# Loading the gate and mix vectors first, longer steps for the softmax sums, and an even pace for the attention

## The chip, the cores and the metric

The kernel runs on 1 core of a Trainium2 chip. Its time is the device time of one execution in microseconds (us); several executions are run and their median is given. All engines of the core work at once: TensorE (PE: matmuls; PEld: its weight loads), VectorE (DVE), ScalarE (ACT), GpSimd (POOL) and SyncE (SP), which in this kernel issues every DMA.

## The reference, cut to what matters

```python
def _attn_ref(q, k, v, cap):                     # 4 batches, 12 heads, 448 positions, 64 wide
    scores = 1.0 / np.sqrt(q.shape[-1]) * np.matmul(q, k.transpose(0, 1, 3, 2))
    scores = cap * np.tanh(scores / cap)
    scores = scores - np.max(scores, axis=-1, keepdims=True)
    attn = np.exp(scores)
    attn = attn / (np.sum(attn, axis=-1, keepdims=True) + 1e-09)
    return np.matmul(attn, v)

def _moe_ref(x, w_val, conv_w, w_out):           # x: 4 x 448 x 768, five taps
    gate = 1.0 / (1.0 + np.exp(-causal_conv(x, conv_w)))
    return gate * (x @ w_val) @ w_out

def _moe2_ref(x, mu_k, mu_r, w_k, w_v, w_r):     # 768 -> 1024 -> 768
    xk = mu_k * x + (1.0 - mu_k) * x_prev
    xr = mu_r * x + (1.0 - mu_r) * x_prev
    k = np.maximum(xk @ w_k, 0.0)
    return 1.0 / (1.0 + np.exp(-(xr @ w_r))) * (k * k @ w_v)

reference = _moe2_ref(_moe_ref(_attn_ref(...)))
```

`causal_conv` stands for the sum over five taps of `conv_w[k] * x` shifted by k positions; `x_prev` is x shifted by one. The weights and `conv_w` arrive as 64-bit numbers, which the kernel narrows to 32 bits.

## The kernel before, in words

**Number format.** Every dense operand is split in two parts, a rounded one and the rest (`split_hi`, `split_lo`), and a product takes three matmuls: high by high, high by low, low by high.

**Attention** goes by pairs of heads, 24 pairs, six per batch. A pair is cut into six pieces (`piece`): piece 0 computes the first two slots of the scores, their tanh and exp, and their sum over slots on GpSimd (`add_up`); piece 1 multiplies the pair before with v (`pv`, copied into `x_f` by ScalarE); pieces 2 and 3 transpose and split the next pair's q and k (`qk_T`, on VectorE or, later, ScalarE and VectorE); piece 4 computes the other two slots; piece 5 adds up the pair before over positions on TensorE (`sums`).

**The chain of the sums.** `sums` (L290) leaves the softmax sums in `rows`; from there they go by DMA into a tile with 128 partitions (`rec<-rows`), VectorE adds a guard (L300) and inverts (L301, `invert`), a DMA writes the reciprocals to DRAM (`recd<-rec`), another reads them back spread over partitions (`R<-recd`, `load_R`), and GpSimd multiplies `x_f` by them (`divide`, L369). Then `x_split` makes the two parts of x, and five taps (`tap`: the first on ScalarE, L379, four on VectorE, L385) and one sigmoid per batch (L389) make the gate. `post(n, ...)` puts each of these n steps later; a step is a piece of attention or a half layer of dense work.

**Order.** Nothing is scheduled at run time: the program's order on each engine is kept (`in_order`). The first 10 pairs run by themselves, with the narrowing and splitting of `w_val` between their pieces (`make_val`). Then the batches go through the dense layers `val` and `out`, 24 half layers of 9 matmuls per batch; behind each half layer the function `behind_first` adds `PACE[b]` to a credit and runs one more piece of attention for each whole credit. The 86 pieces that are left after the first 10 pairs are worked off in this way. Weights of `val`, `out` and `r` are split once, written to DRAM and streamed from there (`wp`), four half layers ahead. With the fourth batch the buffers of the first stage are given back, and `w_k` and `w_v` are made; the second stage is the dense layers `r`, `k`, `v` for each batch.

**Vectors.** `vectors` (L652) loads `conv_w` and the two mix vectors, narrows `conv_w` in five VectorE operations (`narrow`: L444 to L448), transposes all of them on TensorE (`pc`, L666) and copies them to `vecT`. It is called before pair 1. Its tiles come from rings of two buffers, which the slices of the weights use too:

```python
vec = pools["mk"].tile([128, DM], F32, tag="wr", name="vec")[0:8]
c64 = pools["mk"].tile([128, DM, 2], I32, tag="x64", name="c64")
...
make_val(0)
...
for i in range(FIRST):
    if i == 1:
        vectors()
```

## Time and profile before

| what | value |
|---|---|
| time, median of 3 runs (lowest to highest) | 879.13 us (877.95 to 880.84) |
| the profiled execution's own time | 877.56 us |
| its span, first to last instruction | 875.8 us |
| mean granted clock of TensorE | 0.938 |
| busy: PE, PEld, DVE, ACT, POOL | 752.7, 583.8, 480.0, 443.1, 343.6 us |
| instructions | 10699 |
| DMA traffic | 135.50 MB, mean 155 GB/s |
| chain that ended last, by engine | PE 45%, DVE 16%, DMA 16%, ACT 10%, issue 6%, POOL 4%, SPq 2% |

The busy share of an engine over the whole span mixes stages with different limits. The chain that ended last follows the last instruction back to what released it, step by step; a DMA in it is a transfer that something waited for. Where a row shows "idle before" with a releaser, the engine stood still for that long until the one named was done. A matmul's end is modelled, and spans on POOL are rough.

### The profile page before, as it was taken

The page shows a single profiled execution, that of the slowest core. Times are in us where ns is not written, and L with a number is a line of the kernel's source. Part 1 is how long each engine was busy: PE and PEld are TensorE (multiplying, and loading weights), DVE is VectorE, ACT ScalarE, POOL GpSimd, SP SyncE. Part 2 cuts the span into 40 slices and gives each one's busy share as a digit, 9 for nine tenths or more (in the row PEclk, how much of TensorE's full clock was granted, in tenths as well). Part 3 has the DMA queues.
Part 4 walks back from the last instruction along what each step waited for, and adds up shares of the span by engine and source line. Part 5 has one row for each costly group of instructions (what it writes and reads, how often), then busy time and mean ns, then how long its engine had stood idle before and what let it go on. Part 6 is the DMA issues. An engine that isn't in the chain of part 4 may idle for free.

```text
span 875.8 us, 10699 instructions
## 1 busy us (share of the span) xinstructions
PE 752.7 (86%) x3798; PEld 583.8 (67%) x3798; DVE 480.0 (55%) x653; ACT 443.1 (51%) x673; POOL 343.6 (39%) x259
## 2 busy tenths in 40 slices
PE   3676689869789898779899977888999999999996
PEld 2333345536456655545789756768999999999995
DVE  3577887759945746464525756886423332333310
ACT  4475869647575757676232445543443343335311
POOL 2296777636744636576023646774000000000000
PEclk8687879979889999999989999999999999999999
DMA  7264533564647577754668898333720390145001
GB/s 177 66 178 133 148 91 90 140 192 146 205 154 242 182 206 231 236 166 130 209 219 305 292 311 302 108 118 99 229 74 21 85 286 15 43 124 168 1 21 47
DMA packets 148029, 135.50 MB, mean 155 GB/s; under 512 B 78071, under 2 KB 127223, under 8 KB 147966
## 3 DMA queue, kind: packets, MB, share of 16 engines
q1 hardware_dynamic: 147966, 134.72, 51.4%
q8 instruction: 32, 0.52, 0.2%
q14 instruction: 31, 0.25, 0.1%
HBM read 109.35 MB, written 25.25 MB: 154 GB/s over the span
## 4 chain that ended last, share of the span: by engine, by line
PE 45%; DVE 16%; DMA 16%; ACT 10%; issue 6%; POOL 4%; SPq 2%; POOLq 0%; ACTq 0%; DVEq 0%
PE psd L631 37%; PE pv L286 3%; DMA rec<-rows 3%; DVE wr L447 3%; DMA recd<-rec 3%; PE s L244 3%; DVE gate L385 3%; ACT t L246 2%; DVE wr L446 2%; ACT t L253 2%; SPq L142 2%; DMA of<-out 2%; DVE wr L448 1%; DMA wp<-pdout 1%; DMA R<-recd 1%
## 5 line engine op out<-in xcount | busy, mean ns | idle before, releaser
L631 PE MATMUL psd<-blk,wp 128*128 128x448 f32 x1296 | 292.3, 381 | 20.9 <-ACT r L568 6.3
L631 PEld LDWEIGHTS psd<-blk,wp 128*128 128x128 f32 x1296 | 246.6, 194 | 66.5 <-issue 21.3
L631 PE MATMUL psd<-blk,wv 128*128 128x448 f32 x576 | 124.6, 372 | 1.3 <-ACT blk L170 1.1
L170 ACT CAST blk<-f 128x448 fp32r<-128x448 f32 x104 | 59.0, 567 | 128.5 <-DVE f L592 52.8
L631 PE MATMUL psd<-blk,wk 128*128 128x448 f32 x576 | 118.5, 366 | 4.3 <-DVE f L576 4.2
L385 DVE SCALAR_TENSOR_TENSOR gate<-xf,vecT,gate 128x445 f32<-128x445 f32 (+2 forms) x96 | 95.0, 992 | 41.3 <-ACT gate L379 40.7
L631 PEld LDWEIGHTS psd<-blk,wk 128*128 128x128 f32 x576 | 107.9, 188 | 14.3 <-DVE f L576 5.8
L631 PEld LDWEIGHTS psd<-blk,wv 128*128 128x128 f32 x576 | 107.9, 190 | 10.5 <-ACT blk L170 1.4
L175 DVE TENSOR_TENSOR blk<-f,blk 128x448 fp32r<-128x448 f32 x104 | 76.3, 733 | 40.9 <-ACT blk L170 40.8
L271 POOL TENSOR_TENSOR acc<-acc,t 128x896 f32<-128x896 f32 x24 | 54.5, 2271 | 73.5 <-ACT t L253 73.4
L244 PE MATMUL s<-qh,kh 64*128 64x448 f32 x192 | 46.3, 474 | 39.9 <-DVE kh L172 23.9
L246 ACT ACTIVATE t<-s 128x896 f32<-128x896 f32 x72 | 64.0, 917 | 32.0 <-PE s L244 32.0
L253 ACT ACTIVATE t<-t 128x1792 f32<-128x1792 f32 (+1 forms) x48 | 72.5, 1511 | 1.2
L268 POOL TENSOR_TENSOR acc<-t 128x896 f32<-128x896 f32 x24 | 54.2, 2258 | 45.2 <-ACT t L253 27.5
L286 PE MATMUL pv<-t,vn 128*64 128x448 f32 x288 | 70.0, 627 | 0.1
L274 POOL TENSOR_TENSOR acc<-acc,t 64x448 f32<-64x448 f32 x48 | 64.2, 1338 | 3.6
L592 DVE SCALAR_TENSOR_TENSOR f<-of,vecT,prev 128x448 f32<-128x448 f32 x48 | 33.5, 698 | 49.3 <-ACT prev L590 45.8
L244 PEld LDWEIGHTS s<-qh,kh 64*128 64x128 f32 x192 | 19.9, 199 | 59.0 <-issue 19.2
L445 POOL TENSOR_SCALAR wr<-wr 128x384 f32<-128x384 f32 (+1 forms) x28 | 53.5, 1909 | 11.7 <-ACT wr L443 11.6
L576 DVE TENSOR_TENSOR f<-psd,kr 128x448 f32<-128x448 f32 x32 | 19.9, 622 | 61.8 <-ACT kr L574 61.8
L369 POOL TENSOR_TENSOR xf<-xf,R 128x448 f32<-128x448 f32 x24 | 29.5, 1230 | 61.3 <-DMA R<-recd 60.4
L447 DVE SCALAR_TENSOR_TENSOR wr<-x,wr 128x768 int32<-128x768 int32 (+2 forms) x46 | 48.7, 1058 | 1.4
(79 smaller groups left out, 881.1 us busy)
## 6 DMA issues: line engine op xcount, KB each, us to landing
wp<-pdr SPq DMA_DIRECT2D x48, 384.0 KB
wp<-pdval SPq DMA_DIRECT2D x42, 384.0 KB
wp<-pdout SPq DMA_DIRECT2D x36, 384.0 KB
of<-out SPq DMA_DIRECT2D x48, 224.0 KB
x<-in_moe_w_k_dram SPq DMA_DIRECT2D x16, 384.0 KB
x<-in_moe_w_v_dram SPq DMA_DIRECT2D x12, 512.0 KB
qn<-in_q_dram SPq DMA_DIRECT2D x48, 112.0 KB
kn<-in_k_dram SPq DMA_DIRECT2D x48, 112.0 KB
```

Of the source, the lines that this page charges most:

```text
L170: eng.copy(dst, src)
L175: eng.tensor_tensor(dst, src, hi.bitcast(F32), ALU.subtract)
L244: nc.tensor.matmul(ps[:, h], lhsT=a[r, keys[h]], rhs=x[r], start=(m == 0), stop=(m == 2))
L246: nc.scalar.activation(out=t_t[i][:, at:at + 2], in_=ps, func=ACTF.Tanh, scale=reg_t)
L253: nc.scalar.activation(out=a, in_=a, func=ACTF.Exp, scale=reg_e)
L268: eng.tensor_tensor(acc_t[i], t[:, 0:2], t[:, 2:4], ALU.add)
L271: eng.tensor_tensor(acc, acc, t[:, 4:6], ALU.add)
L274: eng.tensor_tensor(acc[r, h], acc[r, h], t[r, 6], ALU.add)
L286: nc.tensor.matmul(ps[64 * h:64 * h + 64], lhsT=w, rhs=t[:, at], start=(n == 0), stop=(n == 3))
L385: eng.scalar_tensor_tensor(g[:, k:], x[:, :S - k], w, g[:, k:], ALU.mult, ALU.add)
L447: lambda: D.scalar_tensor_tensor(mi, hw, -(1 << 30), mi, ALU.bitwise_and, ALU.bitwise_or),
L631: nc.tensor.matmul(ps, lhsT=lhsT, rhs=x[xp], start=(kk == 0 and m == 0), stop=(kk == kb - 1 and m == 2),)
```

## The change

It has three parts.

1. The vectors are loaded after pair 1's q and k and pair 0's v, ahead of pair 2's q, k and v and of the first slice of `w_val`. The five narrowing operations are issued two at a time after the pieces of pair 0, and the transposes after piece 4 of pair 1. The rings of two buffers stay as they are.
2. The chain of the sums: `invert` 5 steps after `sums` instead of 4, `recd<-rec` 7 instead of 6, `R<-recd` 9 instead of 8, `divide` 13 instead of 11, `x_split` 15 instead of 14, the taps from 15 on instead of 13, the sigmoid 20 instead of 18. `rec<-rows` stays at 2.
3. `PACE` is 1.45, 1.45, 1.5 instead of 1.55, 1.55, 3.0.

An assertion is added that a pair is divided when `x_split` takes it; it issues nothing.

```diff
@@ -21,7 +21,7 @@
 
 MAKE_IN = 46
 
-PACE = (1.55, 1.55, 3.0)
+PACE = (1.45, 1.45, 1.5)
 
 SPLIT_AT = (14, 15, 16, 21, 22, 23)
 
@@ -301,8 +301,8 @@
             nc.vector.reciprocal(r, r)
 
         post(2, lambda: dma(out=r, in_=rows[0::64]))
-        post(4, invert)
-        post(6, lambda: dma(out=rec_d[i].rearrange("h s -> (h s)").rearrange("(p n) -> p n", n=NS), in_=r))
+        post(5, invert)
+        post(7, lambda: dma(out=rec_d[i].rearrange("h s -> (h s)").rearrange("(p n) -> p n", n=NS), in_=r))
         prep(*divmod(i, NP))
 
     def shifted(i):
@@ -354,7 +354,7 @@
 
 
     again = [False]
-    x_f, x_R, x_blk, gate_t, gated = {}, {}, {}, {}, set()
+    x_f, x_R, x_blk, gate_t, gated, divided = {}, {}, {}, {}, set(), set()
 
     def prep(b, hp):
 
@@ -367,6 +367,7 @@
 
         def divide():
             nc.gpsimd.tensor_tensor(x_f[i], x_f[i], x_R.pop(i), ALU.mult)
+            divided.add(i)
 
         def tap(k):
             if hp == 0 and k == 0:
@@ -390,14 +391,14 @@
             gated.add((b, again[0]))
 
         if not again[0]:
-            post(8, load_R)
-            post(11, divide)
+            post(9, load_R)
+            post(13, divide)
         if again[0] or b == 0:
-            at(14, x_split, b, hp)
+            at(15, x_split, b, hp)
         for k in range(TAPS):
-            at(13 + k, tap, k)
+            at(15 + k, tap, k)
         if hp == KD - 1:
-            at(13 + TAPS, sigmoid)
+            at(15 + TAPS, sigmoid)
 
     def new_blk():
         return blk_p.tile([128, 2, S], F32R, tag="blk", name="blk")
@@ -412,6 +413,7 @@
         return t[:, 0], t[:, 1]
 
     def x_split(b, hp):
+        assert again[0] or b * NP + hp in divided
         x_blk[b, hp] = split_blk(x_f[b * NP + hp], nc.scalar, engines["PD"[hp % 2]], 0 if again[0] else 1)
 
 
@@ -650,24 +652,28 @@
                 pend.append((b, o))
 
     def vectors():
+
         vec = pools["mk"].tile([128, DM], F32, tag="wr", name="vec")[0:8]
+        ops = []
         if conv_w.dtype == I64:
             c64 = pools["mk"].tile([128, DM, 2], I32, tag="x64", name="c64")
             dma(out=c64[0:TAPS].rearrange("p n two -> p (n two)"), in_=conv_w.bitcast(I32))
+            ops = narrow(c64[0:TAPS], vec[0:TAPS])
         else:
             dma(out=vec[0:TAPS], in_=conv_w)
         dma(out=vec[TAPS:TAPS + 1], in_=mu_k.unsqueeze(0))
         dma(out=vec[TAPS + 1:TAPS + 2], in_=mu_r.unsqueeze(0))
-        if conv_w.dtype == I64:
-            for fn in narrow(c64[0:TAPS], vec[0:TAPS]):
-                fn()
-        pc = ps_m.tile([128, KD, 8], F32, tag="sum", name="pc")
-        for o in range(KD):
-            nc.tensor.transpose(
-                pc[:, o, :TAPS + 2], vec[:TAPS + 2, o * 128:(o + 1) * 128], ident[:TAPS + 2, :TAPS + 2]
-            )
-        nc.vector.tensor_copy(vecT[:, :, :TAPS + 2], pc[:, :, :TAPS + 2])
-        nc.vector.tensor_scalar(mu1, vecT[:, :, TAPS:TAPS + 2], -1.0, 1.0, ALU.mult, ALU.add)
+
+        def turned():
+            pc = ps_m.tile([128, KD, 8], F32, tag="sum", name="pc")
+            for o in range(KD):
+                nc.tensor.transpose(
+                    pc[:, o, :TAPS + 2], vec[:TAPS + 2, o * 128:(o + 1) * 128], ident[:TAPS + 2, :TAPS + 2]
+                )
+            nc.vector.tensor_copy(vecT[:, :, :TAPS + 2], pc[:, :, :TAPS + 2])
+            nc.vector.tensor_scalar(mu1, vecT[:, :, TAPS:TAPS + 2], -1.0, 1.0, ALU.mult, ALU.add)
+
+        return ops, turned
 
 
     stage = ExitStack()
@@ -676,6 +682,7 @@
     dma(out=cap_c, in_=cap.to_broadcast([128, 1]))
     load_qk(1)
     load_v(0)
+    vec_ops, vec_turned = vectors()
     make_identity(nc, ident)
     for p in prev:
         nc.vector.memset(p[:, 0:1], 0.0)
@@ -754,10 +761,14 @@
     make_val(0)
     n_ops, n_done, ticks = 8 * len(order), 0, 0
     for i in range(FIRST):
-        if i == 1:
-            vectors()
         for p in pieces(i):
             piece(*p)
+            if i == 0 and vec_ops:
+                for _ in range(2):
+                    if vec_ops:
+                        vec_ops.pop(0)()
+            if p == (1, 4):
+                vec_turned()
             ticks += 1
             while ops and n_done * MAKE_IN < ticks * n_ops:
                 ops.pop(0)()
```

The lines of the changed kernel are up to 11 further down than those of the kernel before (L445 of before is L447, L559 is L561, L385 is L386, and so on).

On VectorE at the start, from the first operation on the first slice of `w_val` (`wr`) on. `qh`, `ql`, `kh`, `kl` are the parts of pair 1's q and k, `c` is the 64-bit `conv_w`. Before:

```order
L445 TENSOR_SCALAR wr<-wr 128x768
L172 CAST qh<-psq 128x448
L175 TENSOR_TENSOR ql<-psq,qh 128x448
L446 TENSOR_SCALAR wr<-wr 128x768
L172 CAST kh<-psq 128x448
L175 TENSOR_TENSOR kl<-psq,kh 128x448
L447 SCALAR_TENSOR_TENSOR wr<-x_248,wr 128x768
L448 SCALAR_TENSOR_TENSOR wr<-x_248,wr 128x768
L444 TENSOR_SCALAR vec<-c_325 5x768
L445 TENSOR_SCALAR vec<-vec 5x768
L446 TENSOR_SCALAR vec<-vec 5x768
L447 SCALAR_TENSOR_TENSOR vec<-c_325,vec 5x768
```

After:

```order
L446 TENSOR_SCALAR vec<-c_195 5x768
L447 TENSOR_SCALAR vec<-vec 5x768
L447 TENSOR_SCALAR wr<-wr 128x768
L172 CAST qh<-psq 128x448
L175 TENSOR_TENSOR ql<-psq,qh 128x448
L448 TENSOR_SCALAR vec<-vec 5x768
L449 SCALAR_TENSOR_TENSOR vec<-c_195,vec 5x768
L448 TENSOR_SCALAR wr<-wr 128x768
L172 CAST kh<-psq 128x448
L175 TENSOR_TENSOR kl<-psq,kh 128x448
L450 SCALAR_TENSOR_TENSOR vec<-c_195,vec 5x768
L449 SCALAR_TENSOR_TENSOR wr<-x_253,wr 128x768
```

The operations on `vec` stood behind all those on `wr`; now two stand before the first of them, two between `ql` and `kh`, and one behind `kl`.

On VectorE, pair 4's q and k (`qh` to `kl`) and the inversion of pair 1's sums (`rec`). Before:

```order
L172 CAST qh<-psq 128x448
L175 TENSOR_TENSOR ql<-psq,qh 128x448
L447 SCALAR_TENSOR_TENSOR wr<-x_393,wr 128x768
L300 TENSOR_SCALAR rec<-rec,guard 128x7
L301 RECIPROCAL rec<-rec 128x7
L172 CAST kh<-psq 128x448
L175 TENSOR_TENSOR kl<-psq,kh 128x448
L448 SCALAR_TENSOR_TENSOR wr<-x_393,wr 128x768
```

After:

```order
L172 CAST qh<-psq 128x448
L175 TENSOR_TENSOR ql<-psq,qh 128x448
L449 SCALAR_TENSOR_TENSOR wr<-x_384,wr 128x768
L172 CAST kh<-psq 128x448
L175 TENSOR_TENSOR kl<-psq,kh 128x448
L450 SCALAR_TENSOR_TENSOR wr<-x_384,wr 128x768
L300 TENSOR_SCALAR rec<-rec,guard 128x7
L301 RECIPROCAL rec<-rec 128x7
```

The inversion stood between `ql` and `kh`, and now stands behind `kl` and one operation on weights.

On ScalarE at the end of the third batch: the last copies of layer `out` (`f<-psd`), x's last parts (`blk<-xf`), the first taps (`gate<-xf`) and the fourth sigmoid (`gate<-gate`). Before:

```order
L170 CAST blk<-xf 128x448
L563 COPY f<-psd 128x448 x2
L389 ACT_TABLE_LOAD
L389 ACTIVATE gate<-gate 128x2688
L170 CAST blk<-xf 128x448
L563 COPY f<-psd 128x448
L170 CAST blk<-xf 128x448 x2
L563 COPY f<-psd 128x448
L170 CAST blk<-f 128x448 x2
L443 ACTIVATE wr<-x_3930 128x384
```

After:

```order
L170 CAST blk<-xf 128x448
L380 ACTIVATE gate<-xf,vecT 128x448
L565 COPY f<-psd 128x448
L170 CAST blk<-xf 128x448 x2
L565 COPY f<-psd 128x448
L380 ACTIVATE gate<-xf,vecT 128x448
L390 ACT_TABLE_LOAD
L390 ACTIVATE gate<-gate 128x2688
L170 CAST blk<-f 128x448 x2
L445 ACTIVATE wr<-x_3930 128x384
```

The last pair's first tap and the fourth sigmoid stood before the last two copies, and now stand behind the last one, directly ahead of the fourth batch's first operation (`blk<-f`).

## Rows read from the trace of the kernel before

**Rows 1.** Busy time by stage: us, PE, PEld, DVE, ACT, POOL (count), PEclk, DMA share, GB/s.

```profile
31.00:143.00 112.00, 87.07 (x470) 43.63 (x469) 88.28 (x106) 79.56 (x106) 79.00 (x58) 0.82 0.48 130
143.00:262.00 119.00, 97.47 (x499) 63.83 (x498) 83.10 (x96) 80.26 (x112) 68.92 (x53) 0.90 0.55 161
262.00:386.00 124.00, 108.50 (x579) 70.75 (x579) 75.81 (x100) 80.83 (x118) 68.90 (x55) 0.96 0.71 212
386.00:460.00 74.00, 65.81 (x322) 50.04 (x319) 28.76 (x47) 34.10 (x50) 28.20 (x24) 0.95 0.60 184
...
619.00:875.70 256.70, 249.64 (x1266) 230.47 (x1264) 79.86 (x127) 88.67 (x148) 0.00 (x0) 1.00 0.31 94
```

**Rows 2.** Timeline, 12 to 31 us: start, length, engine, line, operation, idle before it.

```profile
15.45 0.89 ACT L443 ACTIVATE wr<-x 128x768 f32<-128x768 f32 x1 [2.17 <-DMA x<-in_moe_w_val_dram]
...
18.50 0.62 DVE L172 CAST kh<-psq 128x448 fp32r<-128x448 f32 x1
...
19.61 2.07 POOL L271 TENSOR_TENSOR acc<-acc,t 128x896 f32<-128x896 f32 x1 [3.39 <-ACT t L253]
...
26.50 0.55 DVE L444 TENSOR_SCALAR vec<-c 5x768 int32<-5x768 int32 x1 [2.21 <-DMA c<-in_moe_conv_w_dram]
...
28.25 0.95 DVE L447 SCALAR_TENSOR_TENSOR vec<-c,vec 5x768 int32<-5x768 int32 x1
...
30.23 0.81 PE L666 MATMUL pc<-ident,vec 7*128 7x7 f32 x6 [16.06 <-DVE vec L448]
...
30.97 0.74 PE L244 MATMUL s<-qh,kh 64*128 64x448 f32 x2
```

**Rows 3.** Timeline, 39 to 42 us: the second slice of w_val, and pair 2's first scores.

```profile
39.45 0.90 ACT L443 ACTIVATE wr<-x 128x768 f32<-128x768 f32 x1
...
41.71 0.48 PE L244 MATMUL s<-qh,kh 64*128 64x448 f32 x2
```

**Rows 4.** Who waited for whom, 31 to 143 us: total us, times, longest.

```profile
PE s L244 <- DVE kh L172: 21.9, 5, 7.7
```

**Rows 5.** Timeline, 62 to 79 us: two inversions and the scores behind the first.

```profile
62.24 0.88 DVE L300 TENSOR_SCALAR rec<-rec,guard 128x7 f32<-128x7 f32 x1 [3.79 <-DMA rec<-rows]
...
63.99 0.74 PE L244 MATMUL s<-qh,kh 64*128 64x448 f32 x2 [5.55 <-DVE kh L172]
...
78.46 2.03 DVE L300 TENSOR_SCALAR rec<-rec,guard 128x7 f32<-128x7 f32 x1
```

**Rows 6.** Timeline at 36 to 41 us; then two lines' durations from 31 to 143 us (ns, min/median/max).

```profile
36.41 2.13 POOL L268 TENSOR_TENSOR acc<-t 128x896 f32<-128x896 f32 x1 [11.12 <-ACT t L253]
...
36.70 2.26 DVE L175 TENSOR_TENSOR wp<-wr,wp 128x384 fp32r<-128x384 f32 x1 [5.21 <-ACT wp L170]
...
40.30 0.55 DVE L175 TENSOR_TENSOR wp<-wr,wp 128x384 fp32r<-128x384 f32 x1
...
L385 DVE SCALAR_TENSOR_TENSOR gate<-xf,vecT,gate x23: 670/1282/1848, 67.9 to 142.6; 128x447 f32<-128x447 f32 x6, 128x446 f32<-128x446 f32 x6, 128x445 f32<-128x445 f32 x6, 128x444 f32<-128x444 f32 x5
...
L274 POOL TENSOR_TENSOR acc<-acc,t x16: 1120/1390/1745, 46.1 to 139.6; 64x448 f32<-64x448 f32 x16
```

**Rows 7.** Who waited for whom, 143 to 386 us (first and second batch).

```profile
POOL xf L369 <- DMA R<-recd: 36.5, 6, 12.4
...
DVE rec L300 <- DMA rec<-rows: 20.4, 6, 9.9
...
PE sum L294 <- DVE ql L175: 11.0, 6, 3.6
...
PE psq L211 <- ACT xf L288: 6.4, 4, 2.7
```

**Rows 8.** Who waited for whom, 386 to 460 us (third batch).

```profile
POOL xf L369 <- DMA R<-recd: 22.2, 3, 12.5
...
PE psd L631 <- DMA wp<-pdout: 5.2, 2, 4.6
```

**Rows 9.** Timeline, 450 to 468 us: the fourth sigmoid.

```profile
453.95 2.45 ACT L389 ACTIVATE gate<-gate 128x2688 f32<-128x2688 f32 x1
```

## The prediction

> **What bounds the kernel now.** I read the table of stages first, then the timeline at the start, then who waited for whom. Of the 875.8 us span, the last 256.7 us (three of the four batches of the second stage) have TensorE busy 249.6 us [rows 1]: 1266 matmuls, 0.197 us each, next to no gap. No edit touches that stretch, so it only moves. What can change lies before it. From 31 to 143 us (attention pairs 1 to 9, up to the first weight matmul) TensorE works 87.1 of 112 us, at a granted clock of 0.82 of full speed; in the first two batches of dense work (143 to 386) 97.5 of 119 and 108.5 of 124; in the third (386 to 460) 65.8 of 74. So TensorE stands idle 25, 37 and 8 us there. A queue in program order makes most of this: an engine waits for one late operand and everything behind it is late too.
>
> The clearest case is the start [rows 2]. Pair 1's key half `kh` is ready at 19.1 us, its low part a little after, yet its score matmuls begin at 30.97. In front of them on TensorE stand the six transposes of `vec`, which waited 16.06 us. `vec` was late because its 64-bit taps take the third buffer of a ring of two: their load could start only when the first slice of `w_val` was narrowed, VectorE stood idle 2.21 us for it, and five operations followed.
>
> **The change, part by part.**
>
> *Vectors first.* The three loads go ahead of pair 2's q and k, the five VectorE operations are spread between pieces of pair 0, and the transposes go behind all scores of pair 1. The slice of `w_val` lands no sooner than the trace shows: ScalarE takes it at 15.45 us [rows 2], with two slices under way; now with one, but three issues later in its queue. I take 15.45 again. By then two of the vector operations are done in idle time. The next two, 0.55 and 0.95 us, come between `ql` and `kh` of pair 1, so `kh` is ready at 19.1 + 1.5 = 20.6 us; GpSimd's sum at 19.61 (2.07 us) can hold the narrowing operation before it for up to another 2.1. Pair 1's scores then start at 20.6 to 22.7 instead of 30.97: 8.3 to 10.3 us sooner. Part comes back. `vec` now keeps one of the two weight buffers until the transposes, so ScalarE's first operation on the second slice (before: 39.45, that is 8.5 us after pair 1 began [rows 3]) waits for them. Pair 1's second scores and its tanh: before, pair 2 began at 41.71, 10.7 us after pair 1; the transposes end about there, and the 0.9 us operation and the tanh behind it come later, so pair 2 is 1.5 to 2 us late. Net 6.5 to 8.5; I take **7.5 us**. The three small loads go ahead of pair 2's on SyncE; that is hidden, since pair 2 is transposed only after pair 1's first scores.
>
> *Sums at longer steps, from 31 to 143 us.* TensorE waited 21.9 us for `kh` in five waits [rows 4]. Two of them contain the inversion, which stood between `ql` and `kh`: at 62.24 VectorE had waited 3.79 us for the sums to land, and the scores started 5.55 us late; at 78.46 the addition took 2.03 us ahead of `kh` [rows 5]. After the change the inversion comes after `kl`, and on SyncE the next pair's `rec<-rows` goes ahead of `R<-recd`, which must wait for the reciprocals' write. So 5.5 + 2.0 = 7.5 us of waits lose their cause. The bounds are 0 (VectorE is as late for another reason) and 25 us, all of TensorE's idle time there. I take 5, nearer to the 7.5 that the rows name, because VectorE has little room: it was busy 88.3 of these 112 us and GpSimd 79.0 [rows 1], and they hold each other up. A split of weights begun at 36.70, inside GpSimd's sum of 36.41, took 2.26 us; the same operation at 40.30 took 0.55 [rows 6].
>
> The Trainium skill (SBUF — State Buffer, section "Who interferes with whom") says that VectorE with two SBUF inputs, or in a mode with two ports, and GpSimd shut each other out for a whole instruction. The trace agrees with the 2.26 beside 0.55. By that rule the shortest durations add up: 23 taps at 0.67, 16 half sums at 1.12, nine sums at 2.13 and eight at 2.07, five narrowings of 3.0 (two operations at 0.55, two at 0.95), ten splits at 0.55: 90 of the 112 us, before GpSimd's divides and copies of v. It would cap this term below 22, where TensorE's idle time allows 25; my 5 stands under both.
>
> *The same steps, 143 to 386 us.* VectorE waited 20.4 us for the sums in six waits and GpSimd 36.5 us for `R` in six [rows 7]; TensorE's waits that follow from this are 11.0 us for `ql` and 6.4 for the `xf` copy, 17.4 of its idle 37. A step (48 half layers and 74 pieces in 243 us) is 2.0 us. One step more on each of the six inversions is 12 of 20.4, a share of 0.59; one more on each divide is 12 of 36.5, 0.33. Between these shares of 17.4, 6 and 10, I take **9 us**, nearer the upper one, since matmuls at the lower clock go with the gaps; the bounds are 0 and 37. The waits behind the first load of `w_out` stay, as nothing in its place changes.
>
> *Pace.* The first two batches take 48 x 0.1 = 4.8 pieces fewer. TensorE's 206 busy us there, less 48 x 9 weight matmuls at 0.197, leave 121 for 74 pieces, 1.6 each; so 7.8 us of matmuls go from there to the third batch: no gain by itself. The third batch then has 16.4 pieces over its first 11 half layers, where it had 12 in 4, and 13 bare half layers instead of 20. Bare ones take weights fastest; the waits for weights were 5.2 us [rows 8]. I take 7/20 of that, **2 us**; bounds: the idle 8.2 us as a gain, 3 as a loss.
>
> *The tail.* The last pair's taps and the fourth sigmoid used to end before the batch did (453.95 [rows 9]). Now they stand behind its last `out` copy: four taps at 0.67 and a sigmoid of 2.45, 5.1 us after ScalarE's own tap. TensorE meanwhile has two accumulators to fill, 36 matmuls or 7.1 us. I cost it at nothing; without that cover it is 5.1.
>
> **Sum.** 7.5 + 5 + 9 + 2 = 23.5 us off the profiled execution's 877.56, so 854.1. That execution is 1.6 below the median of 879.13, so I predict a median of 855.6.
>
> **Rivals.**
> - *Only the start pays.* VectorE and GpSimd are the real limit from 31 us on, and the waits removed come back as waits of one for the other. For it: 167 busy us of two engines in 112, nearly all of VectorE's stretched operations under a GpSimd one. Against it: from 143 on they are less loaded, and GpSimd itself waited 36.5 us for `R`. 877.6 - 7.5 = 870.1, as median 871.6. The port rule of the Trainium skill (same page and section) speaks for this one.
> - *More than I count.* The upper 8.5 us of the start and half of TensorE's idle 25, 37 and 8 us: 43.5, so 834.1, as a median 835.7. For it: TensorE's clock is 0.82 to 0.96 in these stages and rises where gaps go.
> - *Slower: the last chain comes too late.* In the third batch GpSimd waited 22.2 us for `R` in three waits, one of 12.5 [rows 8], behind weight loads on SyncE; 20 bare half layers covered it. Now only 13 remain and the last pair's divide falls due two half layers before the end. It decides if `R` lands more than 7 us late there: then x's last split and the fourth gate hold up the fourth batch's first layer. With all 22.2 us less 7.1 of cover, and terms two to four at nothing: 877.6 - 7.5 + 15.1 = 885.2, 886.8 as a median. Against it: `rec<-rows` now goes earlier in the queue and the inversion has a step more.
> - *The change does not do what it says.* The wait for the transposes only moves to ScalarE's second slice and costs pair 2 what pair 1 gained, and the longer steps merely shift waits: no difference, 879. Against it: the transposes need only pair 1's matmuls, about 10 us after `vec` is ready.
>
> **How the numbers follow.** Forecast 0.58, only the start 0.20, more 0.12, slower 0.06, nothing 0.04. A difference of 0.3% (2.6 us) is about what a measurement of this kernel can tell from none. The first three are faster: 0.90; same 0.04; slower 0.06. The range goes from the third case's time (836) to just past the second's (873), and leaves out slower, nothing, and what of "more" goes beyond it.
>
> **What would show it.** Pair 1's scores start at 20.6 to 22.7 us; the transposes wait for nothing; ScalarE's second slice waits for TensorE. The first weight matmul comes near 130 us instead of 143. TensorE's waits for `kh` fall below 15 us. From 143 to 386, `rec<-rows` and `R<-recd` cost VectorE and GpSimd a third less, and this stretch is some 17 us shorter (9, and 7.8 moved on); the third batch is some 6 longer. The last 257 us keep their length. I am wrong if pair 1 starts after 25 us, if VectorE's stretched operations grow by what TensorE's waits lose, or if the fourth batch begins with TensorE waiting for the gate.

## The result, and the profile after

| | before | changed |
|---|---|---|
| median, us | 879.05 (4 runs, 877.95 to 880.84) | **859.11** (4 runs, 857.54 to 860.01) |
| ratio | 1 | 0.9768, 95% interval 0.9743 to 0.9792 |
| profiled execution: time, span, us | 877.56, 875.8 | 858.79, 857.0 |
| mean granted clock of TensorE | 0.938 | 0.947 |

19.9 us came; 23.5 were forecast. The stages of the changed kernel, in the columns of [rows 1]:

```profile
21.00:131.60 110.60, 83.36 (x474) 42.34 (x474) 92.24 (x106) 76.85 (x101) 83.01 (x61) 0.85 0.53 142
131.60:255.20 123.60, 102.56 (x522) 68.30 (x521) 78.84 (x101) 83.48 (x118) 70.19 (x53) 0.93 0.58 165
255.20:366.60 111.40, 100.46 (x538) 67.60 (x539) 78.67 (x93) 76.17 (x110) 68.32 (x52) 0.94 0.77 227
366.60:437.80 71.20, 66.49 (x337) 48.89 (x334) 31.74 (x49) 33.73 (x54) 31.33 (x27) 0.98 0.65 190
600.00:857.00 257.00, 249.99 (x1268) 230.82 (x1266) 79.82 (x127) 88.44 (x148) 0.00 (x0) 0.99 0.31 94
```

The last 257 us are the same. To say where 18.8 us of span went, I take six marks in both traces: the starts of pair 1's first score matmul, of the first weight matmul, and of ScalarE's sixth, twelfth, eighteenth and last copy of `out` (the ends of the dense batches). The table gives the start, the lengths between marks, and the rest, for every kernel whose profile bears on it (e1 to e9 are explained under the experiments). Each length is of one execution. Two pairs of kernels are the same up to the first weight matmul (before and e3, changed and e4); their first two columns differ by 0.2 to 1.1 us. Whole runs of one kernel spread over 2 to 13 us, and the profiled executions of e1, e2 and e4 are the fastest of theirs (e4's by 3.8 us against its median). So a difference of 1 to 3 us in one length is bookkeeping and not yet an effect.

| kernel | pair 1 | to first weight matmul | batch 1 | batch 2 | batch 3 | batch 4 | rest |
|---|---|---|---|---|---|---|---|
| before | 30.97 | 111.97 | 124.92 | 118.25 | 73.33 | 57.53 | 358.8 |
| changed | 21.09 | 110.55 | 123.51 | 111.46 | 71.17 | 59.40 | 359.8 |
| e1_vectors | 19.85 | 111.63 | 124.77 | 118.18 | 74.77 | 57.27 | 358.2 |
| e2_steps | 30.82 | 109.58 | 122.74 | 110.86 | 75.26 | 54.88 | 358.4 |
| e3_pace | 30.54 | 110.90 | 123.97 | 118.50 | 74.48 | 57.65 | 359.5 |
| e4_no_pace | 19.99 | 110.35 | 122.95 | 110.11 | 73.88 | 55.73 | 359.4 |
| e8_divide | 21.27 | 118.40 | 129.10 | 113.80 | 72.75 | 53.86 | 358.9 |
| e9_invert | 21.25 | 115.48 | 121.16 | 118.40 | 73.58 | 55.91 | 358.3 |

So the change gained 9.9 us at the start, 1.4 up to the first weight matmul, 1.4 and 6.8 in the first two batches, 2.2 in the third, and lost 1.9 in the fourth and 1.0 behind it. The start, from the timeline of the changed kernel (start, length, engine, line, operation, idle before it):

```profile
20.34 0.60 DVE L172 CAST kh<-psq 128x448 fp32r<-128x448 f32 x1
...
21.09 0.74 PE L244 MATMUL s<-qh,kh 64*128 64x448 f32 x2 [6.84 <-DVE kh L172]
...
30.29 0.53 PE L670 MATMUL pc<-ident,vec 7*128 7x7 f32 x6
30.37 0.90 ACT L445 ACTIVATE wr<-x 128x768 f32<-128x768 f32 x1 [1.33 <-DVE wp L175]
...
32.69 0.47 PE L244 MATMUL s<-qh,kh 64*128 64x448 f32 x2
```

Against [rows 2, 3]: pair 1's scores follow `kh` at once, the transposes wait for nothing, pair 2 starts at 32.69 instead of 41.71. Who waited for whom (total us, times, longest), first from 21 to 131.6 us, then from 131.6 to 366.6, which answer to [rows 4] and [rows 7]:

```profile
PE s L244 <- DVE kh L172: 31.7, 6, 9.3
```

```profile
PE psq L211 <- ACT xf L288: 19.1, 6, 5.7
...
DVE rec L300 <- DMA rec<-rows: 16.1, 4, 6.3
...
DVE gate L386 <- ACT gate L380: 8.3, 4, 2.9
...
POOL xf L369 <- DMA R<-recd: 6.3, 4, 3.2
...
PE s L244 <- ACT t L246: 3.1, 1, 3.1
...
PE sum L294 <- DVE ql L175: 0.7, 1, 0.7
```

The waits for `kh` did not fall: 31.7 less pair 1's own 6.84 is 24.9, and before they were 21.9. GpSimd's wait for `R` did, from 36.5 to 6.3; VectorE's for the sums went only from 20.4 to 16.1. Two waits that I had not put among my rows fell too: before, from 143 to 386 us, VectorE waited 31.3 us for the first tap, which ScalarE computes from the divided `xf`, and TensorE 12.8 us for ScalarE's tanh (`t`):

```profile
DVE gate L385 <- ACT gate L379: 31.3, 8, 11.3
...
PE s L244 <- ACT t L246: 12.8, 3, 8.2
```

### The profile page after: what moved, and what is told of

It is laid out like the page before. It is cut to its first block, busy times and chain, and to the rows that moved or that the text cites. A ratio compares the mean times of both kernels' runs of the same rounds, so it can differ in the third digit from the quotient of the medians.

```text
span 857.0 us, 10715 instructions
## 1 busy us (share of the span) xinstructions
PE 748.0 (87%) x3798; PEld 584.0 (68%) x3798; DVE 482.1 (56%) x653; ACT 443.3 (52%) x673; POOL 347.3 (41%) x259
## 4 chain that ended last, share of the span: by engine, by line
PE 47%; DVE 15%; ACT 12%; DMA 12%; issue 6%; POOL 5%; SPq 2%; ACTq 0%; POOLq 0%; DVEq 0%
PE psd L633 38%; PE pv L286 3%; PE s L244 3%; DMA of<-out 3%; DMA wp<-pdout 3%; DVE wr L449 2%; ACT t L246 2%; DVE wr L448 2%; DVE gate L386 2%; DMA qn<-in_q_dram 2%; ACT t L253 2%; SPq L142 2%; DMA recd<-rec 2%; ACT blk L170 1%; PE pso L605 1%
## 5 line engine op out<-in xcount | busy, mean ns | idle before, releaser
L633 PE MATMUL psd<-blk,wp 128*128 128x448 f32 x1296 | 299.5, 386 | 26.5 <-DMA wp<-pdout 9.5
L633 PEld LDWEIGHTS psd<-blk,wp 128*128 128x128 f32 x1296 | 250.3, 198 | 76.5 <-issue 22.2
L633 PEld LDWEIGHTS psd<-blk,wv 128*128 128x128 f32 x576 | 107.7, 190 | 10.5 <-ACT blk L170 1.5
L175 DVE TENSOR_TENSOR blk<-f,blk 128x448 fp32r<-128x448 f32 x104 | 81.7, 786 | 43.7 <-ACT blk L170 43.7
L386 DVE SCALAR_TENSOR_TENSOR gate<-xf,vecT,gate 128x447 f32<-128x447 f32 (+1 forms) x96 | 84.2, 877 | 12.9 <-ACT gate L380 12.3
L286 PE MATMUL pv<-t,vn 128*64 128x448 f32 x288 | 64.5, 586 | 0.0
L447 POOL TENSOR_SCALAR wr<-wr 128x384 f32<-128x384 f32 (+1 forms) x28 | 53.6, 1914 | 17.0 <-ACT wr L445 17.0
L244 PEld LDWEIGHTS s<-qh,kh 64*128 64x128 f32 x192 | 19.1, 190 | 60.3 <-issue 35.1
L578 DVE TENSOR_TENSOR f<-psd,kr 128x448 f32<-128x448 f32 x32 | 19.9, 622 | 62.6 <-ACT kr L576 62.6
L445 ACT ACTIVATE wr<-x 128x768 f32<-128x768 f32 (+2 forms) x46 | 33.2, 722 | 37.2 <-POOL wp L175 17.1
```

The source lines that it names most:

```text
L175: eng.tensor_tensor(dst, src, hi.bitcast(F32), ALU.subtract)
L244: nc.tensor.matmul(ps[:, h], lhsT=a[r, keys[h]], rhs=x[r], start=(m == 0), stop=(m == 2))
L286: nc.tensor.matmul(ps[64 * h:64 * h + 64], lhsT=w, rhs=t[:, at], start=(n == 0), stop=(n == 3))
L386: eng.scalar_tensor_tensor(g[:, k:], x[:, :S - k], w, g[:, k:], ALU.mult, ALU.add)
L447: lambda: engines[engs[1]].tensor_scalar(m, m, WIDE_LO, WIDE_HI, ALU.max, ALU.min),
L633: nc.tensor.matmul(ps, lhsT=lhsT, rhs=x[xp], start=(kk == 0 and m == 0), stop=(kk == kb - 1 and m == 2),)
```

## The experiments

All ratios are to the kernel before, measured together with each (its medians 878.2 to 879.9).

**The parts one by one.** *e1_vectors* is the changed kernel with the old steps and the old pace:

```diff
-PACE = (1.45, 1.45, 1.5)
+PACE = (1.55, 1.55, 3.0)
-        post(5, invert)
+        post(4, invert)
-            post(13, divide)
+            post(11, divide)
-            at(15 + k, tap, k)
+            at(13 + k, tap, k)
```

with `recd<-rec`, `R<-recd`, `x_split` and the sigmoid back likewise. *e2_steps* is the kernel before with the new steps alone, *e3_pace* the kernel before with the new pace alone, *e4_no_pace* the changed kernel with the old pace alone.

> Only the vectors go first; steps and pace are those of before. Theory A (each part has its own waits, and a gain at the start is a mere shift): pair 1 starts at 21 us as in the changed kernel, the first weight matmul comes at 133 to 134 us instead of 142.9, and the time falls by 8 to 10 us, to about 870. Rival B (the old steps give the start back, since the chain of the sums then waits for VectorE at another place): the first weight matmul comes after 139 us, and the time falls by less than 4 us.

> Only the longer steps. Theory A, by the stages of the changed kernel (1.4 us gained after pair 1's start up to the first weight matmul, 8 in the first two batches shared with the pace): the first weight matmul at 141 to 142 us, time lower by 6 to 9 us, about 872. Rival B (VectorE and GpSimd are the limit, and the steps only move waits): lower by less than 3 us. Rival C (the old pace leaves too few steps of attention work between the links): slower than before.

> Only the pace. Theory A: work moves from the first two batches to the third and the rest stays; lower by 0 to 4 us, 875 to 879, with the third batch some 5 us longer. Rival B (the pace, not the steps, is what freed the first two batches): lower by 6 us or more.

> The changed kernel with the old pace. Theory A: 1 to 4 us slower than the changed kernel, 860 to 863, and the first layer of the fourth batch starts without the wait for the gate (1.3 us in the changed kernel). Rival B (the pace carries the gain of the first two batches): 866 or more.

| kernel | median us | ratio, 95% interval |
|---|---|---|
| e1_vectors | 869.20 | 0.9882 (0.9852 to 0.9911) |
| e2_steps | 868.47 | 0.9879 (0.9845 to 0.9914) |
| e3_pace | 878.86 | 0.9991 (0.9972 to 1.0010) |
| e4_no_pace | 858.00 | 0.9771 (0.9734 to 0.9808) |

The vectors are worth 10.4 us, the steps 11.2, together 21.6, which is just what e4 has (879.63 - 858.00). The pace is worth nothing, with the rest or without. In the table of lengths e1 differs from before only in its start, and e2 mainly in batch 2 (7.4 us shorter); no part shortens the stretch up to the first weight matmul by more than 2.4 us. Of the expectations e1's theory A held (the first weight matmul came at 131.48 us, even earlier than named). e2 gained more than any of its theories (11.2 us; A had 6 to 9). e3 met A by its time, but its third batch grew by 1.2 us instead of 5. e4 came out below A's 860 to 863, though, as A had it, its fourth batch did not wait for the gate.

**Which step pays in batch 2.** Based on e4: *e8_divide* keeps only the later divide, split and taps, *e9_invert* only the later inversion and load of `R` (divide and taps keep their old distances behind the load; `x_split` stays at 15), and *e12_taps* has the later inversion and taps but the divide again three steps behind the load.

```diff
e8_divide:
-        post(5, invert)
+        post(4, invert)
-            post(9, load_R)
+            post(8, load_R)
e9_invert:
-            post(13, divide)
+            post(12, divide)
-            at(15 + k, tap, k)
+            at(14 + k, tap, k)
e12_taps:
-            post(13, divide)
+            post(12, divide)
```

> The changed kernel with the old pace, and of the longer steps only those behind the load of R: invert 4, recd<-rec 6, R<-recd 8 as before the change, divide 13, x_split 15, taps from 15. Theory A, what gained in batch 2 is that GpSimd's divide no longer waits for R: batch 2 takes 109 to 113 us (it took 110.1 with all the longer steps, 118.2 with none) and the time is 856 to 862 us. Theory B, the later inversion is what gained, as the prediction had it for two thirds: batch 2 stays at 116 to 119 us and the time is 865 to 870.

> The changed kernel with the old pace, and of the longer steps only those of the inversion: invert 5, recd<-rec 7, R<-recd 9; the divide keeps its 3 steps behind R<-recd (12), x_split 15, taps from 14. Theory A, the divide's wait for R is what counted: it stays, batch 2 takes 116 to 119 us, and the time is 865 to 870 us, like the kernel with the vectors alone (869.2). Theory B, the later inversion is what gained: batch 2 takes 109 to 113 us and the time is 856 to 862.

> The changed kernel with the old pace and the divide one step earlier (12, three steps behind the load of R, as before the change), x_split 15 and the taps from 15 as in the changed kernel, so that three steps instead of two lie between GpSimd's divide and ScalarE's first tap. Theory A, the link that held up batch 2 is the one from the divide through ScalarE's tap to VectorE's taps: batch 2 takes 109 to 113 us, VectorE waits below 6 us for ScalarE's first tap there, and the time is 856 to 862 us, though GpSimd may wait for R again. Theory B, the divide's wait for R itself held it up: batch 2 takes 115 to 119 us, the time is 864 to 869.

Measured: e8 872.27 us (0.9932, 0.9908 to 0.9957), e9 865.08 (0.9843, 0.9819 to 0.9866), e12 854.59 (0.9754, 0.9731 to 0.9777). What each waited for in batch 2, in us:

| kernel | invert, load R, divide, taps at step | GpSimd for R | VectorE for first tap | VectorE for sums | batch 2 |
|---|---|---|---|---|---|
| before | 4, 8, 11, 13 | 20.1 | 23.2 | 15.4 | 118.25 |
| e1_vectors | 4, 8, 11, 13 | 19.0 | 22.4 | 15.1 | 118.18 |
| e3_pace | 4, 8, 11, 13 | 22.9 | 3.5 | 5.1 | 118.50 |
| e9_invert | 5, 9, 12, 14 | 7.3 | 25.4 | 2.6 | 118.40 |
| e12_taps | 5, 9, 12, 15 | 11.7 | 2.6 | 21.0 | 114.13 |
| e8_divide | 4, 8, 13, 15 | none shown | 4.4 | 24.5 | 113.80 |
| changed | 5, 9, 13, 15 | 3.9 | 2.9 | 13.0 | 111.46 |
| e4_no_pace | 5, 9, 13, 15 | 3.2 | 3.6 | 18.3 | 110.11 |
| e2_steps | 5, 9, 13, 15 | 3.8 | 3.2 | 20.6 | 110.86 |

The rows of e9, then of e4, over their second batches:

```profile
DVE gate L386 <- ACT gate L380: 25.4, 4, 11.0
POOL xf L369 <- DMA R<-recd: 7.3, 3, 3.8
...
DVE rec L300 <- DMA rec<-rows: 2.6, 2, 1.8
```

```profile
DVE rec L300 <- DMA rec<-rows: 18.3, 3, 8.4
...
DVE gate L386 <- ACT gate L380: 3.6, 1, 3.6
POOL xf L369 <- DMA R<-recd: 3.2, 1, 3.2
```

My forecast had the wait for the sums as the larger share. It does not set this batch: where it is shortest (2.6 us) the batch is as long as before, and where it is longest (24.5) the batch is 4.4 us shorter. What the long batches share is the chain behind it: `R`, the divide on GpSimd, the first tap on ScalarE, the taps on VectorE. Where those two waits add up to 26 us or more, the batch takes 118; at 14 us, 114; at 7, 110 to 111.5. One kernel stands off this line, e8, with 4.4 us of them and 113.8. Of the kernels described below, e10 (13.5 us, 113.39) and e11 (3.0, 110.87) lie on it, and e13 (8.5, 113.04) lies some 2 us above. A place in e9's timeline where the chain is late at every link:

```profile
360.18 1.13 POOL L369 TENSOR_TENSOR xf<-xf,R 128x448 f32<-128x448 f32 x1 [1.59 <-DMA R<-recd]
...
361.35 0.67 ACT L380 ACTIVATE gate<-xf,vecT 128x448 f32<-128x448 f32 x1 [2.41 <-POOL xf L369]
...
362.05 0.72 DVE L386 SCALAR_TENSOR_TENSOR gate<-xf,vecT,gate 128x447 f32<-128x447 f32 x1 [11.04 <-ACT gate L380]
```

In e4 the pair of 310 us has its tap 3.2 us after the divide is done (311.43, 314.64), and VectorE takes it at 316.84 without waiting.

The cleanest pair is e9 and e12, which differ in one edit, the taps (and the sigmoid) one step later. VectorE's wait for the first tap falls from 25.4 to 2.6 us in batch 2, which is 4.3 us shorter, and from 10.6 to 0.5 in the stretch up to the first weight matmul, which is 109.02 instead of 115.48; the median is 10.5 us lower, with intervals that do not overlap. So the step of the taps is shown to pay. What the divide's step adds (114.13 in e12, 110.11 in e4) rests on two single executions; the medians, 854.59 and 858.00, do not show it.

Of the 8 us in batch 2 between e1 and e4 the later divide and taps alone give 4.4, the later inversion alone none, and the other 3.7 need both. e8 and e12 thus met neither theory in full, and e9 met its theory A by the numbers alone: the wait for `R`, which was to stay, fell from 19.0 to 7.3. e8 lost more ahead of batch 2 (11.1 us against e1 in the two columns before) than the 4.4 it gained in it; up to the first weight matmul TensorE waited 39.5 us for `kh` in it (32.2 in e1), and why was not tried. e12's batch 1 was 2.7 us shorter than e4's and its batch 2 four longer; by its time it is e4 within the spread.

**What bounds the first stage.** *e5_half_sums* takes work away from GpSimd. It leaves out the second half of its sums for the first ten pairs (slots 4 to 6 of 7), so its time stands for a program with less to do:

```diff
-                rest(2, add_up, i, 1)
+                if i >= FIRST:
+                    rest(2, add_up, i, 1)
```

> The changed kernel without the second half of GpSimd's sums (L271 and twice L274, 2.26 and 2 x 1.34 us a pair) for the first 10 pairs: slots 4 to 6 of the 7 are left out of these pairs' softmax sums, so its time stands for a program with less to do. It takes some 40 us of GpSimd's 83 busy us out of the stretch from pair 1's scores to the first weight matmul (110.6 us in the changed kernel). Theory A, VectorE and GpSimd exclude each other and bound that stretch: it falls to 85 to 98 us, the L448 operation of VectorE (128x768, 1440 ns mean) falls towards 1000 ns, the taps (1205 ns) towards 900. Theory B, the stretch is bound by waits in TensorE's queue that have nothing to do with GpSimd: it stays at 105 to 111 us, with GpSimd merely idle for longer.

Measured in one run: 838.79 us, and pair 1's scores to the first weight matmul 93.6 us. Its window, TensorE's waits for `kh` in it, its taps (busy, mean ns), then the taps and one narrowing operation of the changed kernel from 21 to 131.6 us:

```profile
21.50:115.10 93.60, 79.94 (x474) 40.38 (x474) 65.33 (x106) 76.87 (x101) 36.42 (x33) 0.90 0.59 163
```

```profile
PE s L244 <- DVE kh L172: 14.9, 5, 7.5
```

```profile
L386 DVE SCALAR_TENSOR_TENSOR gate<-xf,vecT,gate 128x447 f32<-128x447 f32 (+3 forms) x20 | 13.5, 673 | 0.4 <-ACT gate L380 0.3
```

```profile
L386 DVE SCALAR_TENSOR_TENSOR gate<-xf,vecT,gate 128x447 f32<-128x447 f32 (+3 forms) x20 | 24.1, 1205 | 0.6 <-ACT gate L380 0.5
...
L448 DVE TENSOR_SCALAR wr<-wr 128x768 int32<-128x768 int32 x5 | 7.2, 1440 | 0.1
```

VectorE does the same 106 operations in 65.3 us instead of 92.2, because GpSimd's sums no longer lie across them: a tap takes 673 ns instead of 1205. TensorE's waits for `kh`, behind pair 1's own (7.5), are 7.4 us instead of 24.9. Theory A holds: in this stretch the two engines' mutual stretching is the limit, it reaches TensorE through `kh`, and TensorE, with as many matmuls as before, is 17 us faster through the stretch. The Trainium skill (SBUF — State Buffer, section "Who interferes with whom") has it that a VectorE instruction with two inputs in SBUF contends with a GpSimd instruction that reads SBUF. The taps have two such inputs, and the 673 beside 1205 ns agrees.

**Versions that might be better.** *e10_both* (e4 with the low parts of `w_out` and `w_r` all on VectorE), *e11_longer* (e4 with divide, split and taps one more step later), *e13_sum6* and *e14_sum6_pairs* (slot 6 of the first ten pairs added up by TensorE; e13 on e4, e14 on e11):

```diff
e10_both:
-            wp = w_make(nm, o, a, nc.gpsimd if a else nc.vector)
+            wp = w_make(nm, o, a, nc.vector)
e11_longer:
-            post(13, divide)
+            post(14, divide)
-            at(15 + k, tap, k)
+            at(16 + k, tap, k)
e13_sum6, in sums (GpSimd's two additions of slot 6 left out for i < FIRST):
-            nc.tensor.matmul(ps[64 * h:64 * h + 64], lhsT=ones, rhs=acc[:, h], start=True, stop=True)
+            r = slice(64 * h, 64 * h + 64)
+            nc.tensor.matmul(ps[r], lhsT=ones, rhs=acc[:, h], start=True, stop=i >= FIRST)
+            if i < FIRST:
+                nc.tensor.matmul(ps[r], lhsT=ones[r], rhs=t_t[i][r, 6], start=False, stop=True)
e14_sum6_pairs, the same matmul in a loop of its own behind both halves of acc:
+        for h in range(2 if i < FIRST else 0):
+            r = slice(64 * h, 64 * h + 64)
+            nc.tensor.matmul(ps[r], lhsT=ones[r], rhs=t_t[i][r, 6], start=False, stop=True)
```

> The changed kernel with the old pace, and the low parts of the weights w_out and w_r computed on VectorE alone instead of on GpSimd every other time. In the changed kernel ScalarE waited 17.1 us for such a low part of GpSimd's from 143 to 255 us (a buffer that came free late). Theory A, that wait lies on the path: 850 to 856 us. Theory B, it lies beside other work, and VectorE's added operations (0.55 to 2.3 us each) cost about what they save: 856 to 862 us.

> The changed kernel with the old pace, and one step more behind the load of R: divide 14, x_split 16, taps from 16. Theory A, batch 2 has lost its waits behind GpSimd's divide already (VectorE waited 3.6 us for ScalarE's first tap there, 22.4 with the old steps): nothing more to gain, batch 2 at 108 to 113 us, time 855 to 862. Theory B, each step goes on paying as in the forecast's sum (some 2 us a batch): 850 to 854. Against both stands that the step moves other work in the first stage, as in the kernel with the divide's steps alone, which lost 8 us there: then above 864 with batch 2 still below 113.

> The changed kernel with the old pace; for the first 10 pairs the two half sums of slot 6 (L274, 2 x 1.34 us of GpSimd a pair) are done by two more matmuls a pair in the sums over positions (some 0.5 us each). Theory A, the exclusion of VectorE and GpSimd bounds the stretch from pair 1's scores to the first weight matmul: leaving out 39.5 us of GpSimd's sums made it 17 us shorter, so 24 us of them are worth some 10, less what TensorE's 10 us of new matmuls take back: the stretch takes 99 to 105 us (109.1 without this edit) and the time is 847 to 854 us. Theory B, TensorE's added work costs as much as it frees: 107 to 112 us, time 856 to 862.

> The kernel with the old pace and one step more behind the load of R (848.4 us), and in it slot 6 of the first 10 pairs' sums on TensorE instead of GpSimd, now in the order first half, second half of acc, then first half, second half of slot 6. In the other order each matmul waited for the one before it on the same half, and the sums took 37.7 us of TensorE in 118.5 us instead of 9.5 in 109.3; in this order the two halves ran side by side before (four records in 0.97 us). Theory A, the exclusion of VectorE and GpSimd bounds the stretch up to the first weight matmul (the taps take 1.56 us each in it instead of 0.67): TensorE's addition is 9 to 15 us, GpSimd's loss 24, the taps fall below 1.2 us, the stretch takes 99 to 105 us (107.1 without this edit) and the time is 841 to 847 us. Theory B, the added matmuls stand in TensorE's queue where it was late anyway: 107 to 113 us, 848 to 855.

| kernel | median us | ratio, 95% interval | pair 1 to first weight matmul, us |
|---|---|---|---|
| e10_both | 860.47 | 0.9782 (0.9758 to 0.9807) | 111.45 |
| e11_longer | 848.41 | 0.9661 (0.9639 to 0.9684) | 107.11 |
| e13_sum6 | 862.64 | 0.9798 (0.9767 to 0.9830) | 118.79 |
| e14_sum6_pairs | **844.23** | **0.9607** (0.9583 to 0.9632) | 102.29 |

e10 lands in theory B's range, but it decides nothing: the 17.1 us that ScalarE waited for GpSimd's low parts come with the new pace (17.0 in e3 too), and e4, on which e10 is built, shows no such wait.

e11 beat both its theories: 9.6 us below e4 by the medians, 5.8 by the two profiled spans, of which 3.2 lie ahead of the first weight matmul and the rest is spread over the batches. Its taps take 1556 ns each there, but behind pair 1's own (6.1), TensorE's waits for `kh` are 7.8 us in two instead of 25.0 in five:

```profile
PE s L244 <- DVE kh L172: 13.9, 3, 6.1
PE s L244 <- ACT t L249: 9.4, 3, 6.5
PE s L244 <- ACT t L246: 4.6, 1, 4.6
```

Most of it came back: the scores waited 14.0 us for ScalarE's tanh instead of 1.7, so that both together fell by 4.9 us. This is of one profile, and where the rest of the 9.6 comes from stays open.

e13 fell through its price and met neither theory. (By the marks e4 takes 110.35 us to the first weight matmul, not the 109.1 of the expectation; e13's profile is of its slowest run.) TensorE's sums in e4, in e13, and in e14 (busy us, mean ns of one record):

```profile
L294 PE MATMUL sum<-acc,ones 128*64 128x448 f32 x36 | 9.5, 564 | 1.0 <-DVE vecT L673 1.0
```

```profile
L297 PE MATMUL sum<-t,ones 64*64 64x448 f32 x36 | 18.9, 608 | 0.0
...
L295 PE MATMUL sum<-acc,ones 128*64 128x448 f32 x36 | 18.8, 607 | 1.6 <-DVE vecT L677 1.6
```

```profile
L298 PE MATMUL sum<-t,ones 64*64 64x448 f32 x36 | 9.5, 608 | 0.0
L295 PE MATMUL sum<-acc,ones 128*64 128x448 f32 x36 | 9.4, 600 | 1.6 <-DVE vecT L678 1.6
```

One record is about as long in all three (564 to 608 ns), but the two halves of a pair, which write different halves of the output's partitions, ran side by side in e4 and e14 and one after the other in e13. e13 put each half's second matmul behind its first and paid 28 us where I had reckoned with 10; e14 pays 9.4. The order is shown to set the price, the reason is not: e13's order also changes between matmuls of 128 and of 64 rows three times a pair (`128*64` and `64*64` above), e14's once, and in e13 a matmul of slot 6 and the next half's first one, which stand directly one behind the other and write to different halves, did not overlap either (they start 0.89 us apart). e14's window shows what its order buys:

```profile
20.40:122.70 102.30, 89.08 (x510) 40.71 (x510) 76.38 (x108) 76.91 (x101) 56.88 (x43) 0.91 0.58 155
```

VectorE does 108 operations in 76.4 us (97.2 for 107 in e11), GpSimd has 56.9 instead of 84.1, and the stretch is 4.8 us shorter than e11's. Slot 6 on TensorE is worth 4.2 us by the medians (848.41, 844.23); with the old pace and e11's step, e14 is 14.9 us faster than the changed kernel (859.11).

## Why the prediction was right, point by point

The forecast (855.6, and faster) and its range held, and two of its four terms carry nearly all of the gain (9.9 and 8.2 of 18.8 us). The other two came to next to nothing, and of the two that held one worked by another mechanism than forecast: that its size came out was in part luck. Of the three signs of being wrong that I had named, one came about and one by half.

- **Vectors first, 7.5 us.** It gave 9.9 in the trace and 10.4 alone. `kh`, the scores and the transposes came as named (ready at 20.94, 21.09, no wait). What I took too high is what comes back: 1.5 to 2 us for pair 2, where it was 0.9 (9.9 earlier for pair 1, 9.0 for pair 2). By its own terms the net was 6.3 to 8.8 us, not 6.5 to 8.5. ScalarE's second slice did not wait for the transposes: it started 0.08 us after they began, and the profile puts its wait of 1.33 us on a split of VectorE's.
- **Steps, 31 to 143 us, 5 us.** This step failed: 1.4 came. The waits for `kh` moved to other places and did not fall below 15. The longest, of 9.3 us, ends in the timeline of VectorE below: the operations in front of `kh` are now a tap and a split of x, each at more than twice its shortest time. The rival that VectorE and GpSimd are the real limit was right for this stretch: the taps went from a mean of 1121 to 1205 ns, and the operation L448 (L446 before) from 911 to 1440. That VectorE's stretched operations grow was half of a sign I had named for being wrong (the other half, that TensorE's waits lose as much, did not come: they lost nothing), and e5 shows the cause. VectorE in the changed kernel, then the two groups of the kernel before from 31 to 143 us:

```profile
109.44 1.54 DVE L386 SCALAR_TENSOR_TENSOR gate<-xf,vecT,gate 128x447 f32<-128x447 f32 x1
110.90 1.55 DVE L175 TENSOR_TENSOR blk<-xf,blk 128x448 fp32r<-128x448 f32 x1
112.38 0.61 DVE L172 CAST kh<-psq 128x448 fp32r<-128x448 f32 x1
```

```profile
L385 DVE SCALAR_TENSOR_TENSOR gate<-xf,vecT,gate 128x447 f32<-128x447 f32 (+3 forms) x23 | 25.7, 1121 | 2.4 <-ACT gate L379 2.3
...
L446 DVE TENSOR_SCALAR wr<-wr 128x768 int32<-128x768 int32 x5 | 4.6, 911 | 0.1
```

- **The same steps, 143 to 386, 9 us.** 8.2 came there (9.9 between e1 and e4), so the size held. The reason did not. I took shares of TensorE's waits for `ql` and the `xf` copy, 17.4 us, by what the inversion (0.59) and the divide (0.33) gain. The waits for the sums went from 20.4 to 16.1 and those for `R` from 36.5 to 6.3, with the taps' wait of 31.3 going to 8.3. Of TensorE's two, the wait for `ql` fell from 11.0 to 0.7, but not by VectorE's waits for the sums: over both batches e8 has 30.9 us of those and 2.4 for `ql`, e9 8.2 and 6.2. It goes with the first tap (7.4 in e8, 34.7 in e9). The wait for the `xf` copy grew from 6.4 to 19.1, which is the pace's doing (below).

  One premise was false: "the waits behind the first load of `w_out` stay, as nothing in its place changes". Its place in SyncE's queue changed. Before, then after:

```profile
175.72 0.51 SPq L142 DMA_DIRECT2D R<-recd  x1
176.28 1.61 SPq L142 DMA_DIRECT2D x<-in_moe_w_out_dram  x2
```

```profile
168.19 1.01 SPq L142 DMA_DIRECT2D x<-in_moe_w_out_dram  x2
...
174.57 0.98 SPq L142 DMA_DIRECT2D R<-recd  x1
```

  The load stood behind the load of `R` and now goes ahead of it. ScalarE's wait for it is 10.2 to 12.0 us in the kernels with the old order (before, e1, e8) and 6.5 to 8.0 with the new (changed, e2, e3, e4, e9, e12), and TensorE's wait for the tanh, of which 8.2 us stood behind it, went from 12.8 to 3.1. So the later load of `R` does pay, in batch 1: 121.16 us in e9 against 124.77 in e1 (single executions).
- **Pace, 2 us, and 7.8 us moved to the third batch.** Nothing came: the first two batches were 8.2 us shorter and not 17, and the third 2.2 shorter and not 6 longer. This step failed as well. e3, the pace alone, has the first two batches 0.7 us shorter and the third 1.2 longer. The new pace came with waits of its own: TensorE waited 17.9 us for the `xf` copies in e3 and 19.1 in the changed kernel, 6.4 to 7.1 with the old pace (before, e1, e2, e4), and ScalarE 17.0 and 17.1 us for GpSimd's low parts of weights, a wait that the four do not show. That these ate what fewer pieces freed is read from the rows and was not tried by itself. The row of e3 from 141.4 to 383.9 us:

```profile
PE psq L211 <- ACT xf L288: 17.9, 6, 5.3
```

- **The tail, 0.** The sigmoid did land behind the last copy, and the cover did not quite do. Timeline at the end of the third batch:

```profile
437.78 0.53 ACT L565 COPY f<-psd 128x448 f32<-128x448 f32 x1 [4.73 <-PE psd L633]
438.20 0.67 ACT L380 ACTIVATE gate<-xf,vecT 128x448 f32<-128x448 f32 x1
438.91 2.84 DVE L386 SCALAR_TENSOR_TENSOR gate<-xf,vecT,gate 128x447 f32<-128x447 f32 x4 [3.57 <-ACT gate L380]
441.83 1.28 ACT L390 ACT_TABLE_LOAD   x1 [2.95 <-DVE gate L386]
443.12 2.45 ACT L390 ACTIVATE gate<-gate 128x2688 f32<-128x2688 f32 x1
445.60 0.62 DVE L561 TENSOR_TENSOR f<-psd,gate 128x448 f32<-128x448 f32 x1 [3.85 <-ACT gate L390]
...
446.28 1.89 PE L633 MATMUL psd<-blk,wp 128*128 128x448 f32 x8 [1.29 <-DVE f L561]
```

  I had four taps and the sigmoid at 5.1 us. From the end of ScalarE's tap (438.87) to the end of the sigmoid (445.57) it was 6.7, with the table load of 1.28 that the sum had left out, and TensorE waited 1.29 us. The fourth batch did begin with TensorE waiting for the gate, a sign I had named for being wrong; it cost little. The slower rival named the right place; its price was a quarter of the 5.1 that the text put on a lost cover, and GpSimd's wait for `R`, 13.8 us in the third batch, did not decide it: e4 has 19.6 us of it there and no wait for the gate.

In sum the spans differ by 9.9 + 1.4 + 8.2 + 2.2 - 2.9 = 18.8 us, where 23.5 were forecast: 3.6 less from the second term, 0.8 less from the third, 2.9 lost in and behind the fourth batch (the gate's 1.3 is the part that a row shows), 2.4 more from the start. The 2.2 of the third batch equal the pace's term by chance: e3 shows that the pace is not their cause.

## What to carry to other kernels

A row of waits names the operand that came last, not the one whose delay decides: the wait for the sums here grew by 9 us from e1 to e8 while its batch became 4 shorter. Follow the wait to its last consumer (here the chain divide, tap, taps over three engines), and try each link alone before crediting one. Where two engines stretch each other, moving a wait did little more than move it (24.9 us for `kh` after, 21.9 before); taking work from one of the two, to an engine with idle time, shortened the stretch, and on TensorE the order of the added matmuls set their price. And a longer step moves whatever is issued in order behind it: look at each queue, SyncE's too, before writing that nothing changes there.

## What the hardware showed beside that

- The same 20 taps took 673, 977, 1205 and 1556 ns each in e5, e14, the changed kernel and e11, with GpSimd busy 36 of 94, 57 of 102, 83 of 111 and 84 of 107 us. A duration of VectorE's in this kernel is a price only together with what GpSimd does beside it.
- The sums' matmuls to the two halves of the output's partitions overlapped when issued in turn (four records in 0.97 us, e4 and e14) and did not when a matmul to the same half, of 64 rows instead of 128, came between (two in 0.97, e13): 9.5 against 18.8 us of TensorE for the same 36 records. Which of the two, the half or the rows, keeps them apart the runs do not separate.
